# Rounded products that walk their columns in pieces, with weights at another offset: a set attention with a gated feed-forward on one core

## The chip, the cores and the metric

The kernel runs on one core of one Trainium2 chip. The metric is the device time of one execution in microseconds; the time before is the median of three runs.

## The reference

```python
def mab(q, kv):
    s = scale * (q @ kv.transpose(0, 2, 1))
    s = s - s.max(-1, keepdims=True)
    a = np.exp(s)
    a /= a.sum(-1, keepdims=True) + 1e-09
    return a @ kv
h = mab(I, x)                       # 32 inducing rows against 12480 rows of x, 4 batches
out = mab(x, h)                     # 12480 rows of x against the 32 rows of h
...
h = x @ w_in                        # x: 49920 x 128, w_in: 128 x 2048
g = h * (1.0 / (1.0 + np.exp(-1.702 * h)))
return g @ w_out                    # w_out: 2048 x 128
```

All arrays are float32 (the weights are decoded on chip from 64-bit floats).

## The kernel before

The four batches are cut into six sets of 4 x 512 rows and a rest of 2 x 96. For each batch the kernel computes the 32 rows of `h`, then `h @ w_in` (32 x 2048) in two rounded halves, which stand below each other in a tile `hw`; the softmax weights of 512 rows stand as a high and a low part in a stack `st` of 128 x 512 (`left` for the rests). So the product `x @ w_in` of the feed-forward becomes one matmul of `hw` with `st` for each 128 hidden columns.

The main loop goes over blocks of 512 rows, and in each over eight groups of two hidden chunks (128 each). A group `i` has these parts:

- `hidden(i)`: two first products, weights `hw`, moving columns `st`, into a PSUM tile `ph` of 2 x 512 columns (two such tiles).
- `first(i)`: ScalarE makes `g` from `ph` with the gate; `hi`, `g` rounded to fp32r, is made by ScalarE again from `ph` or by VectorE from `g`; VectorE makes `lo = g - hi`.
- `second(i, c)`: for each chunk three second products into `pso`, in this order: `hi` with `wl`, `lo` with `wh`, `hi` with `wh`, where `wh` and `wl` are the rounded high and low part of `w_out`.

All these operands are fp32r ("rounded products"). In the first eight groups `second` uses plain fp32 instead (`g` with `whole`). The order of everything is fixed when the program is built: a planner (`Clocks`, `Meter`, `Jobs`) keeps a clock of costs per engine and chooses what comes next; the second products run up to 16 chunks behind the first. The attention of the next batch is threaded in between, in tiles `pa`, `e`, `s`, `aT` and a score of small ones (`mx`, `rs`, `m2`, `sm`, `den` and others, from the pool `psm`).

In the first batch the row sets come in the order 4, 6, 3, 0, 5, 5, 2, 1 to the products `pa<-xt,indT_sb`. For sets 4, 3, 0 and 5, whose rows are turned on the chip, these products read their columns by `xg.rearrange("c (k g i) -> c g k i", g=g, i=32)`, that is in 16 runs of 32 columns; for sets 2 and 1 in one run of 512.

Every SBUF tile from the pools on starts where the one before ends. With the sizes before, `st`, `left`, `hw`, `hi`, `lo`, `wh` and `wl` all start at 64 modulo 256 bytes, and every 128-column slice of the weights (512 bytes) does too.

Of the kernel before, what the change touches and what calls it, by code (L numbers as in the profile page):

```python
# [9 lines left out]
F32 = mybir.dt.float32  # L10
I32 = mybir.dt.int32
# [9 lines left out]
P = 128  # L21
# [36 lines left out]
WC = 512  # L58
# [6 lines left out]
S2_LATER = ((0, 6), (1, 2, 3), (4, 5))  # L65
FB = 6
WINDOW = 100.0
CHAIN = 200.0
# [5 lines left out]
class Clocks:  # L74


    def __init__(self):
        self.written, self.read, self.rings, self.before, self.port = {}, {}, {}, {}, {}
        self.halved, self.entered = {}, set()

    def apart(self, t):

        name = t.tensor.name
        self.halved[name] = [f"{name}/{k}" for k in range(-(-t.shape[-1] // WC))]
        return t

    def names(self, ap):
        name = ap.tensor.name
        if name not in self.halved:
            return [name]  # L90
        per = max(1, ap.ap[0][0] // (WC * len(self.halved[name])))
        at = ap.offset % ap.ap[0][0]
# [143 lines left out]


def width(ap):
    return math.prod(ap.shape[1:])
# [3 lines left out]
def set_attention_then_moe(ctx: ExitStack, tc, xT, x, indT, w_in, w_out, outT):  # L243
# [78 lines left out]
    pt = ctx.enter_context(tc.tile_pool(name="pt", bufs=7))  # L322
    pst = ctx.enter_context(tc.tile_pool(name="pst", bufs=G))
    phw = ctx.enter_context(tc.tile_pool(name="phw", bufs=4))
    psm = ctx.enter_context(tc.tile_pool(name="psm", bufs=3))
    ps_h = ctx.enter_context(tc.tile_pool(name="ps_h", bufs=2, space=PSUM))
# [18 lines left out]
    dve.tensor_scalar(mine, rep[:, 0, :], -scale, None, op0=ALU.mult)  # L345
    one = const.tile([1, 1], F32, name="one")
    dve.memset(one, 1.0)
    warm = const.tile([1, 1], F32, name="warm")
    act.activation(warm, one, AF.Exp)
# [3 lines left out]
    w_in_sb = [w_in_all[:, c * WC:(c + 1) * WC] for c in range(NC)]  # L353
    pww = ctx.enter_context(tc.tile_pool(name="pww", bufs=NC // 2))
    whole = {}
    wh = {}
    pwl = ctx.enter_context(tc.tile_pool(name="pwl", bufs=1))
    wl = {}
# [82 lines left out]
    def new_batch(b):  # L441
        a = SimpleNamespace(b=b, s1={}, aTs={}, col={s: k for k, s in enumerate(EARLY + LATE if b == 0 else range(NS))})
        a.mx = psm.tile([P, NS], F32, tag="mx", name="mx", bufs=2)
        a.rs = psm.tile([P, NS], F32, tag="rs", name="rs", bufs=2)
        dve.memset(a.mx, -3.0e38)
        dve.memset(a.rs, 0.0)
        return a
# [72 lines left out]
    def max_scaled(pa):  # L520

        row = psm.tile([P, M], F32, tag="row", name="row", bufs=1)
# [4 lines left out]
        nmx = psm.tile([P, 1], F32, tag="nmx", name="nmx", bufs=2)  # L527
        dve.tensor_reduce(nmx, row, axis=AX.X, op=ALU.add)
        return nmx
# [31 lines left out]
    def spread(rs1):  # L561
        rsb = psm.tile([P, P], F32, tag="rsb", name="rsb", bufs=1)
        dve.tensor_copy(rsb, rs1.broadcast_to([P, P]))
        return rsb
# [7 lines left out]
    def denominators(pa):  # L572
        den = psm.tile([P, M], F32, tag="den", name="den", bufs=1)
        dve.tensor_scalar(den, pa, 1e-9, None, op0=ALU.add)
        dve.reciprocal(den, den)
        return den

    def normalised(b, pa, den):
        hT = psm.tile([P, G, M], F32, tag="hT", name="hT", bufs=1)
# [20 lines left out]
    def second_out(s, pa):  # L600

        t0, g, w = sups[s]
        q = 32 * g
        e, slot = take("e", s)
        k = w // 32
        e = e[:, 0:w].rearrange("p (k m) -> p k m", m=M)
        dve.transpose(e[0:q].rearrange("p k m -> p (k m)"), pa[0:q, 0:w])
        m2 = psm.tile([P, BLK], F32, tag="m2", name="m2")
# [16 lines left out]
    def attention(b):  # L625
# [6 lines left out]
        for pair in S1:  # L632
# [15 lines left out]
            yield from hop(HOPS[1])  # L648
        mx1 = psm.tile([P, 1], F32, tag="mx1", name="mx1", bufs=2)
        dve.tensor_reduce(mx1, a.mx, axis=AX.X, op=ALU.max)  # L650
# [17 lines left out]
        for some in (tuple(range(4)), tuple(range(4, NS))):  # L668
# [14 lines left out]
            for s in some:  # L683
# [7 lines left out]
                yield from hop(HOPS[6])  # L691
        hu = psm.tile([P, P], F32, tag="hu", name="hu", bufs=1)
        dve.tensor_copy(hu, pa[:, 0:P])
        rs1 = psm.tile([P, 1], F32, tag="rs1", name="rs1", bufs=2)
        dve.tensor_reduce(rs1, a.rs, axis=AX.X, op=ALU.add)
# [93 lines left out]
    def hw_tile(b, c):  # L789

        if (b, c // 2) not in hws:
            hws[b, c // 2] = clocks.apart(phw.tile([P, 2 * WC], F32R, tag="hw", name="hw"))
        return hws[b, c // 2][:, c % 2 * WC:(c % 2 + 1) * WC]

# [52 lines left out]
    def normalise(e):  # L847

        q, nb = e.shape[0], e.shape[1]
        sm = psm.tile([P, BLK], F32, tag="sm", name="sm")  # L850
        dve.tensor_reduce(sm[0:q, 0:nb], e, axis=AX.X, op=ALU.add)
# [24 lines left out]
    def start(pf, pw):  # L876
# [3 lines left out]
        }  # L880
        raws["w_out", 0] = clocks.apart(pwl.tile([P, 4 * WC], I32, tag="wl", name="raw"))
        turned = {}
# [84 lines left out]
        def split():  # L967

            for c in range(0, NC, 2):
                out = wholes[c // 2]  # L970
                yield act, [out], has(*SPLIT_AT[c // 2], ("w_out", c), ("w_out", c + 1))
                wh_ = clocks.apart(pww.tile([P, 2 * WC], F32R, tag="w", name="wh"))
                act.copy(wh_, out)
                if c == 0:
                    wls = clocks.apart(pwl.tile([P, DFF], F32R, tag="wl", name="wl"))
                low = wls[:, c * WC:(c + 2) * WC]
# [57 lines left out]
        def maximum(n):  # L1034
            yield dve, [a.mx], has(*[("max", s) for s in (EARLY + LATE)[:n]])
            mx1 = psm.tile([P, 1], F32, tag="mx1", name="mx1", bufs=2)
            dve.tensor_reduce(mx1, a.mx[:, 0:n], axis=AX.X, op=ALU.max)
# [68 lines left out]
        def joining():  # L1106

            yield dve, lambda: [nmxs[ES], nmxs[NS]], has(("nmx", ES), ("nmx", NS), *[("exp", s) for s in EARLY])
            less = psm.tile([P, 1], F32, tag="less", name="less", bufs=1)
            dve.tensor_sub(less, nmxs[NS], nmxs[ES])  # L1110
            rs1 = psm.tile([P, 1], F32, tag="rs1", name="rs1", bufs=2)
            rs2 = psm.tile([P, 1], F32, tag="rs2", name="rs2", bufs=1)
            dve.tensor_reduce(rs1, a.rs[:, 0:ES], axis=AX.X, op=ALU.add)
# [13 lines left out]
            yield dve, [h12, less], has(*[("weighed", s) for s in range(NS)])  # L1127
            hu = psm.tile([P, P], F32, tag="hu", name="hu", bufs=1)
            dve.tensor_scalar(hu, h12[:, 0:P], less, None, op0=ALU.mult)
# [43 lines left out]
        def first_weights():  # L1173
# [15 lines left out]
            chain[0] = True  # L1189
            m2 = psm.tile([P, BLK], F32, tag="m2", name="m2")  # L1190
            dve.tensor_reduce(m2[:, 0:G], pa, axis=AX.X, op=ALU.max)
# [7 lines left out]
        def more_weights(e, slot):  # L1199
# [11 lines left out]
            yield dve, [e], None  # L1211
            m2 = psm.tile([P, BLK], F32, tag="m2", name="m2")
            dve.tensor_reduce(m2[:, G:], far, axis=AX.X, op=ALU.max)
# [84 lines left out]
        jobs.add(first_h_w_in(), rank("hw"))  # L1298
        temps_out = [clocks.apart(pww.tile([P, 2 * WC], U16, tag="w", name="tmp")) for _ in range(2)]
        wholes = [clocks.apart(phw.tile([P, 2 * WC], F32, tag="hw", name="whole")) for _ in range(2)]  # L1300
        for c in range(NC):
# [66 lines left out]
    def hidden(i):  # L1368
# [4 lines left out]
        for c in range(2):  # L1373
            ch = 2 * k + c
            for b, at, w, _ in of:
                pe_.matmul(
                    ph[:, c, at:at + w], hw[b, ch // 4][:, ch % 4 * P:(ch % 4 + 1) * P],
                    st[:, at:at + w], start=True, stop=True,
                )
# [17 lines left out]
    def second(i, c):  # L1397
# [185 lines left out]
```

## Time and profile before

| | |
|---|---|
| median of three runs | 1539.3 us (1538.69 to 1539.86) |
| span of the profiled execution | 1537.2 us, first to last instruction; its own time is given by this span alone, so the part around it is read as the 2.1 us to the median |
| TensorE (matmul) busy | 1529.9 us, 100% |
| TensorE (weight load) busy | 1229.4 us, 80% |
| ScalarE busy | 1345.4 us, 88% |
| VectorE busy | 1301.1 us, 85% |

A matmul's duration in the profile is a latency and overlaps with the next one, so the step from start to start is what the stream costs. Weight loads have rows of their own (PEld) and lie beside the matmul before the one that uses them. L181 is the helper that records each operation, so groups are told apart by their tiles: `pso<-hi,wl` is the tile written, the moving operand and the weights.

### The profile page before, as it was taken

The page shows a single profiled execution, that of the slowest core. Times are in us where ns is not written, and L with a number is a line of the kernel's source. Part 1 is how long each engine was busy: PE and PEld are TensorE (multiplying, and loading weights), DVE is VectorE, ACT ScalarE, POOL GpSimd, SP SyncE. Part 2 cuts the span into 40 slices and gives each one's busy share as a digit, 9 for nine tenths or more (in the row PEclk, how much of TensorE's full clock was granted, in tenths as well). Part 3 has the DMA queues.
Part 4 walks back from the last instruction along what each step waited for, and adds up shares of the span by engine and source line. Part 5 has one row for each costly group of instructions (what it writes and reads, how often), then busy time and mean ns, then how long its engine had stood idle before and what let it go on. Part 6 is the DMA issues. An engine that isn't in the chain of part 4 may idle for free.

```text
span 1537.2 us, 21743 instructions
## 1 busy us (share of the span) xinstructions
PE 1529.9 (100%) x7736; PEld 1229.4 (80%) x7736; DVE 1301.1 (85%) x1512; ACT 1345.4 (88%) x1549; POOL 0.7 (0%) x6
## 2 busy tenths in 40 slices
PE   9999999999999999999999999999999999999999
PEld 6588878877888887877787887887788888888887
DVE  7988888789788887789789888778978888888886
ACT  4899989898999888889999888989899998888884
POOL 0000000000000000000000000000000000000000
PEclk9999999999999999999999999999999999999999
DMA  8210157713051115833133110872301101101100
GB/s 335 74 50 25 49 205 124 215 40 101 31 206 42 35 35 97 180 104 102 42 102 131 39 49 14 158 200 57 97 23 40 48 25 37 49 24 40 48 26 20
DMA packets 83849, 127.53 MB, mean 83 GB/s; under 512 B 12320, under 2 KB 50848, under 8 KB 77856
## 3 DMA queue, kind: packets, MB, share of 16 engines
q1 hardware_dynamic: 83600, 126.05, 28.8%
q8 instruction: 63, 1.03, 0.3%
q14 instruction: 42, 0.34, 0.1%
q10 hardware_dynamic: 144, 0.10, 0.0%
HBM read 72.11 MB, written 25.56 MB: 64 GB/s over the span
## 4 chain that ended last, share of the span: by engine, by line
PE 97%; DMA 1%; DVE 0%; ACT 0%; issue 0%; SPq 0%
PE pso L181 69%; PE ph L181 23%; PE pa L181 4%; DMA xt<-in_xT 1%; PE h L181 0%; ACT g L181 0%; PE spun L1268 0%; DMA hw<-tl 0%; DVE e L181 0%; DVE m L181 0%; DVE sm L181 0%; DVE two L181 0%; SPq L196 0%; DVE hw L181 0%; DVE w_in_all L181 0%
## 5 line engine op out<-in xcount | busy, mean ns | idle before, releaser
L181 DVE TENSOR_TENSOR lo<-g,hi 128x1024 fp32r<-128x1024 f32 x776 | 938.0, 1216 | 136.1 <-ACT hi L181 121.8
L181 ACT ACTIVATE g<-ph 128x1024 f32<-128x1024 f32 (+1 forms) x784 | 812.8, 1042 | 153.8 <-PE ph L181 74.7
L181 PE MATMUL pso<-hi,wl 128*128 128x512 f32 (+1 forms) x1552 | 603.7, 389 | 0.0
L181 PE MATMUL pso<-lo,wh 128*128 128x512 f32 (+1 forms) x1552 | 602.4, 388 | 0.0
L181 PE MATMUL pso<-hi,wh 128*128 128x512 f32 (+1 forms) x1552 | 602.3, 388 | 0.0
L181 ACT ACTIVATE hi<-ph 128x1024 fp32r<-128x1024 f32 (+1 forms) x493 | 512.6, 1040 | 0.0
L181 PE MATMUL ph<-st,hw 128*128 128x512 f32 x1536 | 474.9, 393 | 1.1 <-ACT g L181 1.1
L181 PEld LDWEIGHTS ph<-st,hw 128*128 128x128 f32 x1536 | 285.8, 188 | 77.0 <-issue 9.1
L181 PEld LDWEIGHTS pso<-hi,wl 128*128 128x128 f32 x1552 | 291.4, 188 | 62.8 <-issue 2.5
L181 PEld LDWEIGHTS pso<-hi,wh 128*128 128x128 f32 x1552 | 291.2, 188 | 59.6
L181 PEld LDWEIGHTS pso<-lo,wh 128*128 128x128 f32 x1552 | 291.4, 188 | 59.1
L181 DVE CAST hi<-g 128x1024 fp32r<-128x1024 f32 (+1 forms) x283 | 193.5, 684 | 73.8 <-ACT g L181 73.4
L181 ACT COPY ob<-pso 128x512 f32<-128x512 f32 (+1 forms) x98 | 60.0, 612 | 11.1 <-PE pso L181 11.1
L181 ACT ACT_TABLE_LOAD x26 | 33.4, 1283 | 1.2 <-PEq L1573 0.7
L181 PE MATMUL pa<-xt,indT_sb 128*32 128x512 f32 x200 | 24.9, 599 | 0.5 <-DMA xt<-in_xT 0.4
L181 ACT ACTIVATE s<-s,nmx 128x512 f32<-128x512 f32 (+1 forms) x27 | 17.8, 662 | 4.1 <-DVE nmx L181 4.0
L181 PE MATMUL pa<-xt,hT 128*32 128x512 f32 (+1 forms) x176 | 21.3, 593 | 0.0
L181 DVE TENSOR_TENSOR e<-e,sm 128x512 f32<-128x512 f32 (+3 forms) x29 | 17.8, 612 | 1.0
L181 DVE TENSOR_REDUCE m<-e 128x16 f32<-128x512 f32 (+2 forms) x28 | 17.3, 619 | 1.0
L181 DVE STREAM_TRANSPOSE aT<-s 128x512 f32<-128x512 f32 (+1 forms) x28 | 17.8, 640 | 0.2
L181 DVE TENSOR_REDUCE sm<-e 128x16 f32<-128x512 f32 (+3 forms) x29 | 17.3, 596 | 0.4 <-ACT e L181 0.4
L181 DVE TENSOR_TENSOR e<-e,m 128x512 f32<-128x512 f32 (+2 forms) x28 | 17.3, 617 | 0.0
(120 smaller groups left out, 356.9 us busy)
## 6 DMA issues: line engine op xcount, KB each, us to landing
xt<-in_xT SPq DMA_DIRECT2D x44, 1024.0 KB, 7.6
out_T<-ob SPq DMA_DIRECT2D x96, 256.0 KB, 2.0
xn<-in_x SPq DMA_DIRECT2D x72, 256.0 KB, 7.1
st<-ahT SPq DMA_DIRECT2D x184, 64.0 KB, 2.0
st<-alT SPq DMA_DIRECT2D x184, 64.0 KB, 2.0
raw<-in_w_in SPq DMA_DIRECT2D x4, 512.0 KB, 10.8
xf<-in_x SPq DMA_DIRECT2D x2, 1024.0 KB, 17.4
raw<-in_w_out SPq DMA_DIRECT2D x4, 512.0 KB, 15.3
```

What stands on the lines that cost most here:

```text
L181: return f(*a, **k)
```

## The change

Three things are changed, and no operation is added or taken away.

1. The rounded products of `hidden` and `second` get another access pattern, `by_lines`, for the moving columns and for the output alike: pieces of 4 columns (16 bytes), each fourth piece in turn, so columns 0-3, 16-19, 32-35, ... to the end, then 4-7, 20-23, ..., four passes in all. Column k of the output still belongs to column k of the input. The plain fp32 products keep the single run.
2. The weight tiles `hw`, `wh` and `wl` get 4 spare columns (16 bytes) at either end, and the pools stand in another order. In the built program `hi` and `lo` start at 224 modulo 256, `st` and `left` at 0, the weights in `wh` and `wl` at 16, those in `hw` at 48. Thus `hi` and `lo` against `wh` and `wl`, and `st` against `hw`, lie 208 bytes behind modulo 256; `hi` against `hw` lies at 176, and `st` against `wl` at 240.
3. The small tiles come from several pools that stand between the larger ones, with as many buffers of each as before. `hw` is now one tile of 2048 columns per batch and two such tiles, instead of four of 1024.

```diff
+LINES = (4, 4)
+ASIDE = 4
+SMALL = {"m2": "psm1", "less": "psm2", "rs2": "psm4", "row": "psm4", "mx": "psm4", "den": "psm5", "rs": "psm5", "sm": "psm6"}
...
+def by_lines(ap):
+
+    return ap.rearrange("p (n s i) -> p s n i", s=LINES[0], i=LINES[1])
...
-    pst = ctx.enter_context(tc.tile_pool(name="pst", bufs=G))
-    phw = ctx.enter_context(tc.tile_pool(name="phw", bufs=4))
-    psm = ctx.enter_context(tc.tile_pool(name="psm", bufs=3))
...
+    pool_of("phw0")
+    pool_of("psm1", 3)
+    pst = pool_of("pst", G)
+    pool_of("psm2")
+    pool_of("phw1")
+    pool_of("psm3", 2)
+    pool_of("pw0")
+    pool_of("psm4", 2)
+    pool_of("pw1")
+    pool_of("psm5", 2)
+    pool_of("pwl")
+    pool_of("psm6", 3)
+    pools["psm5"].tile([P, 8], F32, tag="aside", name="aside", bufs=1)
...
+    def aside(pool, tag, name, n):
+        t = clocks.apart(pools[pool].tile([P, n * WC + 2 * ASIDE], F32R, tag=tag, name=name), ASIDE)
+        return t[:, ASIDE:ASIDE + n * WC]
...
-        if (b, c // 2) not in hws:
-            hws[b, c // 2] = clocks.apart(phw.tile([P, 2 * WC], F32R, tag="hw", name="hw"))
-        return hws[b, c // 2][:, c % 2 * WC:(c % 2 + 1) * WC]
+        if b not in hws:
+            hws[b] = aside(f"phw{b % 2}", f"hw{b % 2}", "hw", 4)
+        return hws[b][:, c * WC:(c + 1) * WC]
...
-                wh_ = clocks.apart(pww.tile([P, 2 * WC], F32R, tag="w", name="wh"))
+                wh_ = aside(f"pw{c // 2}", f"w{c // 2}", "wh", 2)
...
-                    wls = clocks.apart(pwl.tile([P, DFF], F32R, tag="wl", name="wl"))
+                    wls = aside("pwl", "wl", "wl", 4)
...
                 pe_.matmul(
-                    ph[:, c, at:at + w], hw[b, ch // 4][:, ch % 4 * P:(ch % 4 + 1) * P],
-                    st[:, at:at + w], start=True, stop=True,
+                    by_lines(ph[:, c, at:at + w]), hw[b, ch // 4][:, ch % 4 * P:(ch % 4 + 1) * P],
+                    by_lines(st[:, at:at + w]), start=True, stop=True,
                 )
...
-            pe_.matmul(o, wlc, hi[:, c, :], start=(ch == 0), stop=False)
-            pe_.matmul(o, whc, lo[:, c, :], start=False, stop=False)
-            pe_.matmul(o, whc, hi[:, c, :], start=False, stop=last)
+            out, high, low = by_lines(o), by_lines(hi[:, c, :]), by_lines(lo[:, c, :])
+            pe_.matmul(out, wlc, high, start=(ch == 0), stop=False)
+            pe_.matmul(out, whc, low, start=False, stop=False)
+            pe_.matmul(out, whc, high, start=False, stop=last)
```

The change moves no instruction on any engine. TensorE's order in the main loop, before (tile written, moving operand and weights, then the output's shape):

```order
L181 MATMUL pso<-hi,wh 128x512
L181 MATMUL ph<-st,hw 128x512 x2
L181 MATMUL pso<-hi,wl 128x512
L181 MATMUL pso<-lo,wh 128x512
L181 MATMUL pso<-hi,wh 128x512
L181 MATMUL pso<-hi,wl 128x512
```

The same place of the change:

```order
L185 MATMUL pso<-hi,wh 128x4x32x4
L185 MATMUL ph<-st,hw 128x4x32x4 x2
L185 MATMUL pso<-hi,wl 128x4x32x4
L185 MATMUL pso<-lo,wh 128x4x32x4
L185 MATMUL pso<-hi,wh 128x4x32x4
L185 MATMUL pso<-hi,wl 128x4x32x4
```

Only the shape differs (and the line of the recording helper): 512 columns are now 4 passes of 32 pieces of 4 columns.

## Rows read from the trace of the kernel before

**Rows 1.** The page's parts 1 and 2: busy times, and the granted TensorE clock.
```profile
PE 1529.9 (100%) x7736; PEld 1229.4 (80%) x7736; DVE 1301.1 (85%) x1512; ACT 1345.4 (88%) x1549; POOL 0.7 (0%) x6
...
PEclk9999999999999999999999999999999999999999
```
**Rows 2.** The page's part 4: the chain that ended last, shares by engine and line.
```profile
PE 97%; DMA 1%; DVE 0%; ACT 0%; issue 0%; SPq 0%
PE pso L181 69%; PE ph L181 23%; PE pa L181 4%; DMA xt<-in_xT 1%; PE h L181 0%; ACT g L181 0%; PE spun L1268 0%; DMA hw<-tl 0%; DVE e L181 0%; DVE m L181 0%; DVE sm L181 0%; DVE two L181 0%; SPq L196 0%; DVE hw L181 0%; DVE w_in_all L181 0%
```
**Rows 3.** Groups by form: names, shapes, count, busy us, mean ns, idle before.
```profile
L181 PE MATMUL pso<-hi,wl 128*128 128x512 f32 x1520 | 592.9, 390 | 0.0
...
L181 PE MATMUL ph<-st,hw 128*128 128x512 f32 x1536 | 474.9, 393 | 1.1 <-ACT g L181 1.1
...
L181 PE MATMUL pso<-hi,wl 128*128 128x384 f32 x32 | 10.8, 338 | 0.0
...
L181 PE MATMUL ph<-left,hw 128*128 128x192 f32 x64 | 9.4, 269 | 0.0
```
**Rows 4.** Pieces of the chain: start us, us, what.
```profile
1124.87 6.80 PE pso L181 x30
```
**Rows 5.** Timeline of a plain stretch: start us, us, engine, operation.
```profile
1240.06 0.39 PE L181 MATMUL pso<-lo,wh 128*128 128x512 f32 x1
...
1240.28 0.39 PE L181 MATMUL pso<-hi,wh 128*128 128x512 f32 x1
...
1240.51 0.39 PE L181 MATMUL pso<-hi,wl 128*128 128x512 f32 x1
1240.51 0.19 PEld L181 LDWEIGHTS pso<-lo,wh 128*128 128x128 f32 x1
1240.74 0.39 PE L181 MATMUL pso<-lo,wh 128*128 128x512 f32 x1
```
**Rows 6.** Timeline of TensorE in the last block, twenty products of 384 columns.
```profile
1527.02 0.33 PE L181 MATMUL pso<-lo,wh 128*128 128x384 f32 x1
...
1530.31 0.33 PE L181 MATMUL pso<-hi,wh 128*128 128x384 f32 x1
```
**Rows 7.** Timeline of TensorE, plain fp32 second products in the first groups.
```profile
63.53 2.74 PE L181 MATMUL pso<-g,whole 128*128 128x512 f32 x6
65.70 1.02 PE L181 MATMUL ph<-st,hw 128*128 128x512 f32 x2
66.56 1.02 PE L181 MATMUL pso<-g,whole 128*128 128x512 f32 x2
67.02 1.04 PE L181 MATMUL ph<-st,hw 128*128 128x512 f32 x2
```
**Rows 8.** Timeline of TensorE in the first batch: set 4, then set 2.
```profile
8.31 1.07 PE L181 MATMUL pa<-xt,indT_sb 128*32 128x512 f32 x8
...
22.55 1.07 PE L181 MATMUL pa<-xt,indT_sb 128*32 128x512 f32 x8 [0.43 <-DMA xt<-in_xT]
```
**Rows 9.** Timeline of TensorE, first products of a rest, 192 columns each.
```profile
1519.80 0.59 PE L181 MATMUL ph<-left,hw 128*128 128x192 f32 x4
1520.22 0.41 PE L181 MATMUL pso<-hi,wl 128*128 128x512 f32 x1
```
**Rows 10.** Busy times by stretch: us, PE, PEld, DVE, ACT, POOL, clock, DMA share, GB/s.
```profile
140.00:210.00 70.00, 70.00 (x319) 55.60 (x318) 58.15 (x71) 65.54 (x76) 0.00 (x0) 1.00 0.35 125
...
1200.00:1300.00 100.00, 100.00 (x442) 82.52 (x441) 86.83 (x90) 91.03 (x102) 0.00 (x0) 1.00 0.14 40
1400.00:1500.00 100.00, 100.00 (x443) 82.81 (x442) 87.61 (x99) 84.95 (x96) 0.00 (x0) 1.00 0.10 32
```
**Rows 11.** Waits: who waited for whom, us in total, times, longest us.
```profile
ACT g L181 <- PE ph L181: 74.7, 107, 2.4
...
PEld ph L181 <- ACT g L181: 6.6, 8, 1.4
```

More of the change, by code (lines that the diff above doesn't have):

```diff
@@ L78, in __init__, with apart @@
         self.written, self.read, self.rings, self.before, self.port = {}, {}, {}, {}, {}
-        self.halved, self.entered = {}, set()
-    def apart(self, t):
+        self.halved, self.entered, self.aside = {}, set(), {}
+    def apart(self, t, aside=0):
         name = t.tensor.name
-        self.halved[name] = [f"{name}/{k}" for k in range(-(-t.shape[-1] // WC))]
+        self.aside[name] = aside
+        self.halved[name] = [f"{name}/{k}" for k in range(-(-(t.shape[-1] - 2 * aside) // WC))]
         return t
@@ L91, in names @@
         per = max(1, ap.ap[0][0] // (WC * len(self.halved[name])))
-        at = ap.offset % ap.ap[0][0]
+        at = ap.offset % ap.ap[0][0] - self.aside[name] * per
         end = (at + sum(step * (n - 1) for step, n in ap.ap[1:])) // per
@@ L322, in set_attention_then_moe, with pool_of, small @@
     pt = ctx.enter_context(tc.tile_pool(name="pt", bufs=7))
-    pst = ctx.enter_context(tc.tile_pool(name="pst", bufs=G))
-    phw = ctx.enter_context(tc.tile_pool(name="phw", bufs=4))
-    psm = ctx.enter_context(tc.tile_pool(name="psm", bufs=3))
+    pools = {}
+    def pool_of(name, bufs=1):
+        pools[name] = ctx.enter_context(tc.tile_pool(name=name, bufs=bufs))
+        return pools[name]
+    pool_of("phw0")
[11 more added lines that the diff above has]
+    pools["psm5"].tile([P, 8], F32, tag="aside", name="aside", bufs=1)
+    def small(shape, tag, name, **k):
+        return pools[SMALL.get(tag, "psm3")].tile(shape, F32, tag=tag, name=name, **k)
+    def aside(pool, tag, name, n):
+        t = clocks.apart(pools[pool].tile([P, n * WC + 2 * ASIDE], F32R, tag=tag, name=name), ASIDE)
+        return t[:, ASIDE:ASIDE + n * WC]
     ps_h = ctx.enter_context(tc.tile_pool(name="ps_h", bufs=2, space=PSUM))
@@ L345, in set_attention_then_moe @@
     dve.tensor_scalar(mine, rep[:, 0, :], -scale, None, op0=ALU.mult)
-    one = const.tile([1, 1], F32, name="one")
+    ones = const.tile([1, 2], F32, name="ones")
+    one, warm = ones[:, 0:1], ones[:, 1:2]
     dve.memset(one, 1.0)
-    warm = const.tile([1, 1], F32, name="warm")
     act.activation(warm, one, AF.Exp)
@@ L353, in set_attention_then_moe @@
     w_in_sb = [w_in_all[:, c * WC:(c + 1) * WC] for c in range(NC)]
-    pww = ctx.enter_context(tc.tile_pool(name="pww", bufs=NC // 2))
     whole = {}
     wh = {}
-    pwl = ctx.enter_context(tc.tile_pool(name="pwl", bufs=1))
     wl = {}
@@ L442, in new_batch @@
         a = SimpleNamespace(b=b, s1={}, aTs={}, col={s: k for k, s in enumerate(EARLY + LATE if b == 0 else range(NS))})
-        a.mx = psm.tile([P, NS], F32, tag="mx", name="mx", bufs=2)
-        a.rs = psm.tile([P, NS], F32, tag="rs", name="rs", bufs=2)
+        a.mx = small([P, NS], tag="mx", name="mx", bufs=2)
+        a.rs = small([P, NS], tag="rs", name="rs", bufs=2)
         dve.memset(a.mx, -3.0e38)
@@ L520, in max_scaled @@
     def max_scaled(pa):
-        row = psm.tile([P, M], F32, tag="row", name="row", bufs=1)
+        row = small([P, M], tag="row", name="row", bufs=1)
         dve.tensor_reduce(
@@ L526, in max_scaled @@
         dve.tensor_mul(row, row, mine)
-        nmx = psm.tile([P, 1], F32, tag="nmx", name="nmx", bufs=2)
+        nmx = small([P, 1], tag="nmx", name="nmx", bufs=2)
         dve.tensor_reduce(nmx, row, axis=AX.X, op=ALU.add)
@@ L561, in spread @@
     def spread(rs1):
-        rsb = psm.tile([P, P], F32, tag="rsb", name="rsb", bufs=1)
+        rsb = small([P, P], tag="rsb", name="rsb", bufs=1)
         dve.tensor_copy(rsb, rs1.broadcast_to([P, P]))
@@ L572, in denominators @@
     def denominators(pa):
-        den = psm.tile([P, M], F32, tag="den", name="den", bufs=1)
+        den = small([P, M], tag="den", name="den", bufs=1)
         dve.tensor_scalar(den, pa, 1e-9, None, op0=ALU.add)
@@ L578, in normalised @@
     def normalised(b, pa, den):
-        hT = psm.tile([P, G, M], F32, tag="hT", name="hT", bufs=1)
+        hT = small([P, G, M], tag="hT", name="hT", bufs=1)
         dve.tensor_mul(
@@ L607, in second_out @@
         dve.transpose(e[0:q].rearrange("p k m -> p (k m)"), pa[0:q, 0:w])
-        m2 = psm.tile([P, BLK], F32, tag="m2", name="m2")
+        m2 = small([P, BLK], tag="m2", name="m2")
         yield e, slot
@@ L648, in attention @@
             yield from hop(HOPS[1])
-        mx1 = psm.tile([P, 1], F32, tag="mx1", name="mx1", bufs=2)
+        mx1 = small([P, 1], tag="mx1", name="mx1", bufs=2)
         dve.tensor_reduce(mx1, a.mx, axis=AX.X, op=ALU.max)
@@ L691, in attention @@
                 yield from hop(HOPS[6])
-        hu = psm.tile([P, P], F32, tag="hu", name="hu", bufs=1)
+        hu = small([P, P], tag="hu", name="hu", bufs=1)
         dve.tensor_copy(hu, pa[:, 0:P])
-        rs1 = psm.tile([P, 1], F32, tag="rs1", name="rs1", bufs=2)
+        rs1 = small([P, 1], tag="rs1", name="rs1", bufs=2)
         dve.tensor_reduce(rs1, a.rs, axis=AX.X, op=ALU.add)
@@ L849, in normalise @@
         q, nb = e.shape[0], e.shape[1]
-        sm = psm.tile([P, BLK], F32, tag="sm", name="sm")
+        sm = small([P, BLK], tag="sm", name="sm")
         dve.tensor_reduce(sm[0:q, 0:nb], e, axis=AX.X, op=ALU.add)
@@ L880, in start @@
         }
-        raws["w_out", 0] = clocks.apart(pwl.tile([P, 4 * WC], I32, tag="wl", name="raw"))
+        raws["w_out", 0] = clocks.apart(pools["pwl"].tile([P, 4 * WC], I32, tag="wl", name="raw"))
         turned = {}
@@ L1035, in maximum @@
             yield dve, [a.mx], has(*[("max", s) for s in (EARLY + LATE)[:n]])
-            mx1 = psm.tile([P, 1], F32, tag="mx1", name="mx1", bufs=2)
+            mx1 = small([P, 1], tag="mx1", name="mx1", bufs=2)
             dve.tensor_reduce(mx1, a.mx[:, 0:n], axis=AX.X, op=ALU.max)
@@ L1108, in joining @@
             yield dve, lambda: [nmxs[ES], nmxs[NS]], has(("nmx", ES), ("nmx", NS), *[("exp", s) for s in EARLY])
-            less = psm.tile([P, 1], F32, tag="less", name="less", bufs=1)
+            less = small([P, 1], tag="less", name="less", bufs=1)
             dve.tensor_sub(less, nmxs[NS], nmxs[ES])
-            rs1 = psm.tile([P, 1], F32, tag="rs1", name="rs1", bufs=2)
-            rs2 = psm.tile([P, 1], F32, tag="rs2", name="rs2", bufs=1)
+            rs1 = small([P, 1], tag="rs1", name="rs1", bufs=2)
+            rs2 = small([P, 1], tag="rs2", name="rs2", bufs=1)
             dve.tensor_reduce(rs1, a.rs[:, 0:ES], axis=AX.X, op=ALU.add)
@@ L1127, in joining @@
             yield dve, [h12, less], has(*[("weighed", s) for s in range(NS)])
-            hu = psm.tile([P, P], F32, tag="hu", name="hu", bufs=1)
+            hu = small([P, P], tag="hu", name="hu", bufs=1)
             dve.tensor_scalar(hu, h12[:, 0:P], less, None, op0=ALU.mult)
@@ L1189, in first_weights @@
             chain[0] = True
-            m2 = psm.tile([P, BLK], F32, tag="m2", name="m2")
+            m2 = small([P, BLK], tag="m2", name="m2")
             dve.tensor_reduce(m2[:, 0:G], pa, axis=AX.X, op=ALU.max)
@@ L1211, in more_weights @@
             yield dve, [e], None
-            m2 = psm.tile([P, BLK], F32, tag="m2", name="m2")
+            m2 = small([P, BLK], tag="m2", name="m2")
             dve.tensor_reduce(m2[:, G:], far, axis=AX.X, op=ALU.max)
@@ L1298, in start @@
         jobs.add(first_h_w_in(), rank("hw"))
-        temps_out = [clocks.apart(pww.tile([P, 2 * WC], U16, tag="w", name="tmp")) for _ in range(2)]
-        wholes = [clocks.apart(phw.tile([P, 2 * WC], F32, tag="hw", name="whole")) for _ in range(2)]
+        temps_out = [
+            clocks.apart(pools[f"pw{k}"].tile([P, 2 * WC], U16, tag=f"w{k}", name="tmp")) for k in range(2)
+        ]
+        both = clocks.apart(pools["phw1"].tile([P, 4 * WC], F32, tag="hw1", name="whole"))
+        wholes = [both[:, 2 * k * WC:2 * (k + 1) * WC] for k in range(2)]
         for c in range(NC):
```

## The prediction

> **What bounds the kernel now.** I read the page's busy times first. TensorE is busy for the whole span and its granted clock is full, 2.4 GHz, in all forty slices [rows 1]. That alone says little, because matmul ends are modelled. So I went on to the chain that ended last: 97% of the span lies on TensorE, 69% on the second products into `pso` and 23% on the first products into `ph` [rows 2]. The forms behind those shares are few: 1520 of 512 columns for each of the three second products, 1536 first products, 32 of each second product with 384 columns, and 64 first products with 192 [rows 3]. That makes 4560 + 96 + 1536 + 64 = 6256 rounded products, and they are what the change touches.
>
> The mean of one (390 ns) is a latency. What counts is the step from one start to the next, and the timeline and the chain show it. Thirty second products of 512 columns take 6.80 us on the chain [rows 4], so 226.7 ns each, and the single starts agree: 1240.06, 1240.28, 1240.51, 1240.74 [rows 5]. The rows also show which load runs beside which product: with the product by `wl` starts the load of `wh` for the product after it. At 384 columns the starts go from 1527.02 to 1530.31 in 19 steps, 173.2 ns each [rows 6]. The two steps differ by 53.5 ns for 128 columns, 0.418 ns a column, which is one column per 2.4 GHz cycle (0.417 ns). So 512 columns need 213.3 ns and **13.3 ns of each step do not depend on the columns**: 32 column times. One weight load brings 128 columns of 4 bytes, 512 bytes, or 32 pieces of 16 bytes. One lost column per piece would give just this number. That is a reading, not a proof.
>
> A second row speaks for it. Each plain fp32 product `pso<-g,whole` has two records, and each has 512 columns. Six records need 2.17 us up to the next first product, two need 0.46 [rows 7]: (2.17 - 0.46)/4 = 427.5 ns, and two streams of 512 columns would take 426.7. About 1 ns is left over (up to 3 ns by the rounding of the starts), though a load of the same 512 bytes runs below each. So a load beside a stream need not cost 13 ns. It does where the stream takes a new column in each cycle.
>
> **The change, part by part.** The order of instructions and their waits stay on all engines; no DMA is added or moved. Three things are left.
>
> (1) The addresses. Before, all rounded operands start at the same place modulo 256, so the stream and the load beside it walk from the same offset. Now the columns lie 208 bytes behind the weights. But the load beside a product is that of the next one. By the order of the program, 4787 products have a load at 208 beside them, 717 (from `hi` with `wh` to `hw`) at 176, and 708 (from `st` or `left` with `hw` to `wl`) at 240. The other 44 stand ahead of smaller jobs.
>
> (2) The walk: 128 pieces of 4 columns in place of one run of 512, on the reading and on the writing side.
>
> (3) Small tiles in other places, with as many buffers as before. I cost this at nothing: no engine waits for them on the chain [rows 2], and if a small tile came late, its chain has the other products of the order as cover.
>
> The price of (1) and (2) together is in no row. The bounds for a step: all 13.3 ns gone (no stall left) on the one side. On the other side, a loss: if every one of the 128 pieces costs one column time more, 128 x 0.417 = 53 ns are added. The nearest row for a stepped walk is in the first batch: the products `pa<-xt,indT_sb` of set 4 read their columns in 16 runs of 32, those of set 2 in one run, and eight records need 1.07 us in both cases [rows 8]. That speaks for zero on the reading side, but with runs eight times as long, in fp32, and with an unbroken output. For the stall itself the nearest row is the fp32 pair, with 1 to 3 ns left over [rows 7]. So I take 2 ns as the rest for the 4787 products at 208: 4787 x 11.3 ns = 54 us. For the 717 + 708 at other offsets I know only 0 to 13.3 and take half: 1425 x 6.7 ns = 9.5 us. The 64 products of 192 columns give nothing either way; four of them take 0.42 us, 105 ns each [rows 9], more than their 80 ns of streaming, so the load sets their pace. (They also show that a load can follow a load after 105 ns; at 215 ns a step the loads are no bound.) Together 63.5 us.
>
> What is late next? ScalarE is busy 65.5 of 70 us in the stretch with the largest share, 93.6%, and 91.0 and 85.0 of 100 in the plain stretches behind [rows 10]. All 13.3 ns would shrink a stretch by 5.9%, my forecast by 4.5%. So ScalarE has room in each, but little in the first. It also waits for `ph` now, 74.7 us in all, and gets part of that back [rows 11]. Against that, the loads for `ph` wait 6.6 us for ScalarE's `g` [rows 11], and this grows when TensorE comes sooner. I add 6 us, about as much again; the bounds I keep are 0 and 20 us, three times the 6.6.
>
> The sum: -54 - 9.5 + 6 = -57.5 us. The profiled execution's span is 1537.2, 2.1 us under the median of 1539.3; I take those 2.1 us as unchanged. 1539.3 - 57.5 = **1482 us**.
>
> **Two rules of the skill against this.** In [rows 5] the load and the stream overlap and the step is 13.3 ns longer than the stream. The Trainium skill ("TensorE: Matmul & The Clock Gate", Step-by-step: what each phase is for) says that the stream and the weight load have SBUF read ports of their own, so that a load takes nothing from the running product. By that rule addresses cannot matter and the sum would be 0 us; the 13.3 ns next to the 1 ns of the fp32 pair speak against it, but do not show that an address is the reason.
>
> The second bears on the writing side. All outputs of TensorE in this trace are unbroken runs. The Trainium skill ("Advanced Engine Details and Errata", PSUM Cachelines) says that an access pattern that is not contiguous in PSUM slows matmuls significantly, and also that two neighbouring elements should be contiguous for the best rate. By its first half this change loses; by its second, runs of four are enough. No row here shows either.
>
> **The rivals.**
> - *Nothing moves.* The 13.3 ns belong to a rounded product or to its load at any address. For it: they are the same at 384 and 512 columns, and every pair in this trace has the same offset, so none shows another price. Against it: the fp32 pair. Time: 1539.
> - *A part.* Other offsets still meet, only at other moments: a third to a half of the stall goes. 6192 x 4.4 to 6.7 ns = 27 to 41 us; with few new waits some 1500 to 1515.
> - *All of it.* 6192 x 13.3 = 82 us, 1457, and with 6 us of waits 1463.
> - *Slower: the broken writes.* Each run of 4 columns in PSUM (or each step to another piece in SBUF) costs one column time. 6192 x 53.3 ns = 330 us; even if the stall goes as forecast, 1539 + 330 - 64 = 1805. For it: no output in this trace is broken. Against it: [rows 8], for the reading side. The point that decides is low: 10.3 ns of mean gain over 128 pieces is 0.08 ns a piece, a fifth of a column time. A whole column time for each piece is likely, if there is any cost; between, little.
>
> **How the numbers follow.** Most of the stall gone (1463 to 1500): 0.50, because the number 32 and the fp32 pair both point to the load meeting the stream. A part (1500 to 1536): 0.27. Nothing: 0.09. Slower: 0.14. About 0.2% (3 us) is what a measurement of this kernel can tell from no change. So faster 0.77, same 0.09, slower 0.14. The range goes from 1460, all of the stall gone and few new waits, up to 1541, which takes in the case of no change; it leaves out the slower case and a little below. The likeliest case alone has 1463 to 1500.
>
> **What would show it.** In the changed profile, runs of `pso` on the chain should show about 215 ns a product (30 in 6.45 us) where they had 6.80, and the 384-column steps about 162 ns. The pairs at 176 and 240 can be read apart: the step from `hi` with `wh` to `ph`, and from `ph` to `wl`. ScalarE's waits for `ph` should shrink from 74.7 us and TensorE's waits for `g` grow by a few. Wrong would be: a step that still has 226.7 (no contention by address); one that grows with the columns by over 0.418 ns (the walk costs per piece); or steps of 215 with the time lost again in waits for ScalarE.

## The result and the profile after

The changed kernel takes 1517.5 us (median of 4 runs, 1517.05 to 1518.42) against 1539.2 us (median of the four runs of the kernel before beside them): 21.7 us less, ratio 0.986 (95% interval 0.9845 to 0.9873). The forecast was 1482. The sign was right, the size was 2.6 times too large.

The busy times of the changed kernel, against [rows 1], and its chain, against [rows 4]:

```profile
PE 1507.8 (99%) x7736; PEld 1226.8 (81%) x7736; DVE 1300.5 (86%) x1512; ACT 1343.5 (89%) x1549; POOL 0.7 (0%) x6
```

```profile
1109.31 6.63 PE pso L185 x30
```

The work of VectorE and ScalarE is the same to 2 us, and TensorE has 22 us less. Thirty second products on the chain need 6.63 us, 221.0 ns each, where they had 226.7. That is less than half of the 13.3 ns of each step that do not depend on the columns. The timeline of a plain stretch (start us, us, engine, operation; TensorE alone) shows where the rest goes, against [rows 5]:

```profile
1243.53 0.38 PE L185 MATMUL pso<-hi,wl 128*128 128x512 f32 x1
1243.75 0.38 PE L185 MATMUL pso<-lo,wh 128*128 128x512 f32 x1
1243.97 0.38 PE L185 MATMUL pso<-hi,wh 128*128 128x512 f32 x1
1244.19 0.38 PE L185 MATMUL pso<-hi,wl 128*128 128x512 f32 x1
1244.41 0.38 PE L185 MATMUL pso<-lo,wh 128*128 128x512 f32 x1
1244.63 0.39 PE L185 MATMUL pso<-hi,wh 128*128 128x512 f32 x1
1244.85 0.62 PE L185 MATMUL ph<-st,hw 128*128 128x512 f32 x2
1245.32 0.38 PE L185 MATMUL pso<-hi,wl 128*128 128x512 f32 x1
```

Between second products the starts step by 0.22. The two first products together take 0.47, 1244.85 to 1245.32, where two steps of before are 0.45. So the second products gained and the first products lost. The table is taken from all starts of the two traces, by what a step goes from and to, with the offset of the pair in brackets (means over all steps, the few long waits included):

| step, 512 columns | count | before, ns | after, ns | difference, us |
|---|---|---|---|---|
| second to second product (208) | 3850 | 227.3 | 221.0 | -24.3 |
| second to first (176) | 710 | 226.9 | 225.6 | -1.0 |
| first to first (208) | 800 | 236.0 | 236.7 | +0.6 |
| first to second (240) | 693 | 227.1 | 231.8 | +3.3 |
| products of 384 and 192 columns, others | | | | -0.2 |
| sum | | | | -21.6 |

The sum is the difference of the spans, 1537.2 - 1515.5 = 21.7 us. The means hide how even the steps are. Of 808 products by `wl` that follow another second product, 798 step by 220 ns. In a group of the usual form the step from the last second product to `ph` is 226, from the first `ph` to the second 229, from there to `wl` 232 or 233, and the one after that 218. In cycles of 2.4 GHz 220.0 ns is 528: 16 above the 512 columns, where 226.7 was 32 above.

The products of 384 columns, against [rows 6]:

```profile
1505.09 0.33 PE L185 MATMUL pso<-lo,wh 128*128 128x384 f32 x1
...
1508.25 0.33 PE L185 MATMUL pso<-hi,wh 128*128 128x384 f32 x1
```

19 steps in 3.16 us are 166.3 ns (173.2 before): again some 16 column times above 160.0. The walk in pieces adds nothing per column.

### The profile page after: what moved, and what is told of

It reads as the page before. It is cut to its first block, busy times and chain, and to the rows that moved or that the text cites. A ratio compares the mean times of both kernels' runs of the same rounds, so it can differ in the third digit from the quotient of the medians.

```text
span 1515.5 us, 21743 instructions
## 1 busy us (share of the span) xinstructions
PE 1507.8 (99%) x7736; PEld 1226.8 (81%) x7736; DVE 1300.5 (86%) x1512; ACT 1343.5 (89%) x1549; POOL 0.7 (0%) x6
## 4 chain that ended last, share of the span: by engine, by line
PE 98%; DVE 1%; DMA 1%; ACT 0%; issue 0%; SPq 0%
PE pso L185 69%; PE ph L185 24%; PE pa L185 4%; PE h L185 0%; PE spun L1299 0%; DMA xt<-in_xT 0%; ACT g L185 0%; DMA hw<-tl 0%; DVE e L185 0%; DVE sm L185 0%; ACT s L185 0%; DVE m L185 0%; DVE two L185 0%; DVE aT L185 0%; DVE hw L185 0%
## 5 line engine op out<-in xcount | busy, mean ns | idle before, releaser
L185 PE MATMUL pso<-hi,wh 128*128 128x512 f32 (+1 forms) x1552 | 593.8, 383 | 0.0
L185 PE MATMUL pso<-hi,wl 128*128 128x512 f32 (+1 forms) x1552 | 590.2, 380 | 0.0
L185 PE MATMUL pso<-lo,wh 128*128 128x512 f32 (+1 forms) x1552 | 589.6, 380 | 0.0
```

The lines of the kernel that those rows point to most:

```text
L185: return f(*a, **k)
```

## The experiments

Six kernels ran. Three are the kernel with one part of the change altered, three are rounded products alone, to price a step without anything beside it.

**A sweep of walks and offsets** (`sweep`). A step is the time from one product's start to the next. The offset is the number of bytes, modulo 256, by which the columns lie behind the weights that are loaded beside them; a walk is the order in which a product reads its columns. The core of it:

```diff
+    def group(k, s, i, d, how="both"):
+        mv = m[:, d // 4:d // 4 + 512]
...
+        for r in range(N):
+            c = r % 4
+            nc.tensor.matmul(b, w[:, c * P:(c + 1) * P], a, start=(r == 0), stop=(r == N - 1))
```

> This kernel computes nothing of the reference: it runs only rounded products of 512 columns, 16 in a row for each setting, all from one weight tile and one column tile. It steps the columns' offset behind the weights from 0 to 240 bytes modulo 256 in steps of 16, for nine walks: one run of 512, then pieces of 4 columns taken each 2nd, 4th, 8th, 16th and 32nd, pieces of 8 taken each 4th, pieces of 16 taken each 2nd and each 4th; and, for pieces of 4 taken each 4th, the same walk on the reading side alone and on the writing side alone. Theory A (the stream and the load beside it meet at addresses modulo 256): at offset 0 one run gives 226.7 ns a step as in the kernel before, pieces of 4 taken each 4th at 208 give 220 ns as in the second products after the change, and for both walks the step changes by several ns with the offset; writing alone in pieces changes nothing. Theory B (the walk alone sets the step): within a walk all offsets give the same, 226.7 for one run and 220 for pieces of 4 taken each 4th, and the part of the walk that matters can be the writing side.

Mean of the last 12 steps of each setting, in ns, from the starts in the trace. The first setting, one run at offset 0, began at the lower of the clock's two levels, 1.2 GHz, with steps of 427 ns, and is left out; its value is that of the setting "written in pieces, read in one run", which reads the same.

```
offset       0     16    32    48    64    80    96    112   128   144   160   176   192   208   224   240
one run      228.6 231.7 233.2 233.3 229.7 231.2 234.2 231.1 231.7 233.3 233.9 231.1 233.3 234.4 233.3 226.7
4, each 4th  223.3 224.4 224.9 222.3 220.0 230.0 230.0 228.2 230.0 224.2 226.6 223.5 227.4 220.0 226.7 229.9
```

For the other walks, the lowest and the highest of their 16 offsets: pieces of 4 taken each 2nd 231.1 to 233.4, each 8th 240.0 to 249.7, each 16th 276.5 to 279.8, each 32nd 264.8 to 270.8; pieces of 8 each 4th 224.4 to 235.2; pieces of 16 each 2nd 230.0 to 242.2, each 4th 232.7 to 239.2. Reading in pieces and writing in one run gives the second line again, within 0.1 ns at 15 of 16 offsets (at 32 it gave 220.8 for 224.9). Writing in pieces and reading in one run gives the first line at all 15 that can be compared.

So Theory A holds and B falls: offset and walk both count, the step goes from 220.0 to 280 ns, and 64 and 208 share the floor. The four slices of the weights lie 512 bytes apart and step alike at 64 and 208; that 256 bytes more make no difference was not tried by itself. **What lies on the writing side costs nothing** in this walk: pieces of 16 bytes in PSUM, each 4th in turn, read 0.0 ns longer than one run. The rival that ended slower falls here, by its own mechanism; its price of one column time per piece would have been 53 ns. The Trainium skill ("Advanced Engine Details and Errata", PSUM Cachelines) says both that a non-contiguous pattern slows matmuls and that two neighbours should be contiguous. This trace agrees with the second: runs of four show 0.0 ns. Shorter runs were not tried on the writing side alone.

**The walk alone** (`walk_alone`), the kernel before with `by_lines` and nothing else:

```diff
-                    ph[:, c, at:at + w], hw[b, ch // 4][:, ch % 4 * P:(ch % 4 + 1) * P],
-                    st[:, at:at + w], start=True, stop=True,
+                    by_lines(ph[:, c, at:at + w]), hw[b, ch // 4][:, ch % 4 * P:(ch % 4 + 1) * P],
+                    by_lines(st[:, at:at + w]), start=True, stop=True,
...
+            out, high, low = by_lines(o), by_lines(hi[:, c, :]), by_lines(lo[:, c, :])
```

> The kernel before with the walk of the change alone; all offsets stay 0. Theory A (address and walk together): the step of the second products is not 220 ns, and the first products are equal to the second, since all pairs have one offset; the time lies anywhere from 1505 to 1560 us. Theory B (walk alone): second products at 220 ns, and the first products as slow as in the changed kernel (229 and 232 ns), so 1517 us.

Measured: 1534.7 us, ratio 0.997 (0.9958 to 0.9978). Its nine times spread over 4.3 us (1531.1 to 1535.4), those of before over 1.8. Pieces of the chain and starts in the timeline:

```profile
753.32 6.81 PE pso L181 x30
...
389.64 6.79 PE pso L181 x30
```

```profile
1241.43 0.39 PE L181 MATMUL pso<-hi,wl 128*128 128x512 f32 x1
1241.66 0.38 PE L181 MATMUL pso<-lo,wh 128*128 128x512 f32 x1
1241.88 0.39 PE L181 MATMUL pso<-hi,wh 128*128 128x512 f32 x1
...
1243.01 0.40 PE L181 MATMUL pso<-hi,wh 128*128 128x512 f32 x1
1243.25 0.39 PE L181 MATMUL pso<-hi,wl 128*128 128x512 f32 x1
```

Thirty products need as long as before, 227 ns each, but the steps are uneven: 0.23, 0.22, 0.24. The walk alone is worth 4.4 us. First and second products are alike, as Theory A had it: 226 ns in the mean from second to second, to the first and back (between two first products 234 ns, and 236 in the kernel before, waits included).

The starts in the trace show more than the mean. The steps run in one of two repeating orders, and one order holds for hundreds of products:

```
815.8 us on, 581 steps, mean 223.3    218 230 224 221 218 230 224 221 219 230 224 221 ...
448.8 us on, 575 steps, mean 226.6    220 222 221 234 239 225 226 220 222 221 234 239 225 226 ...
```

Some 4800 of 6040 steps are in the order of seven (226.7), some 1000 in the order of four (223.3, the sweep's value for this walk at 0). What chooses between them was not found.

**The offsets alone** (`offset_alone`), the changed kernel with

```diff
-    return ap.rearrange("p (n s i) -> p s n i", s=LINES[0], i=LINES[1])
+    return ap
```

> The changed kernel with its addresses, but each product reads and writes one run of 512 columns. Theory A in the form that the offset alone removes the stall: 1517 us, second products at 220 ns. Theory B: 226.7 ns in all and 1539 us. Between: a step that differs with the pair, 208, 176 and 240.

Measured: 1576.9 us, ratio 1.025 (1.0232 to 1.0262), slower than either kernel. Both expectations missed: neither the gain nor no change. The chain:

```profile
772.71 7.00 PE pso L185 x30
```

233.3 ns a step. The sweep's first line has it: one run at 208 gives 234.4, and only at 0 and 240 does it come to 226.7 (at 0 after some nine products). The kernel before stood at one of the two best of the 16 offsets for one run. So the two parts do not add: walk -4.4, offsets +37.9, both -21.7 us.

**All pairs at 208** (`all_208`). 32 bytes of small tiles move, so the stack starts at 224 and the weights in `hw` at 16:

```diff
     pool_of("psm3", 2)
+    pools["psm3"].tile([P, 8], F32, tag="more", name="more", bufs=1)
...
-    pools["psm5"].tile([P, 8], F32, tag="aside", name="aside", bufs=1)
+    spare = pools["psm5"].tile([P, 8], F32, tag="aside", name="aside", bufs=1)
...
-    ones = const.tile([1, 2], F32, name="ones")
+    ones = spare[0:1, 0:2]
```

> The changed kernel with 32 bytes moved, so that the stack starts at 224 and the first products' weights at 16 modulo 256: now every stream lies 208 bytes behind the weights loaded beside it, also at the changes from second to first products and back, which lie at 176 and 240 in the changed kernel. Theory A (the pair's offset sets the step): the three steps round a pair of first products (225.6, 229.0 and 232.3 ns in the changed kernel) come to 220 to 221 each, some 25 ns for each of 700 pairs, 17 us: about 1500 us. Rival (a change of the tile read, or the first write of a bank, costs this at any offset): the three steps stay as they are, 1517 us.

Measured: 1500.1 us (1499.9 to 1501.4), ratio 0.975 to the kernel before (0.9735 to 0.9764), 17.4 us below the changed kernel. Busy times, chain, and the same stretch of the timeline:

```profile
PE 1491.9 (99%) x7736; PEld 1227.8 (82%) x7736; DVE 1299.9 (87%) x1512; ACT 1342.4 (90%) x1549; POOL 0.7 (0%) x6
```

```profile
738.81 6.60 PE pso L185 x30
```

```profile
1243.51 0.38 PE L185 MATMUL pso<-hi,wl 128*128 128x512 f32 x1
...
1244.61 0.38 PE L185 MATMUL pso<-hi,wh 128*128 128x512 f32 x1
1244.83 0.60 PE L185 MATMUL ph<-st,hw 128*128 128x512 f32 x2
1245.27 0.38 PE L185 MATMUL pso<-hi,wl 128*128 128x512 f32 x1
```

The two first products now take 0.44 us instead of 0.47, and 220 ns is the common step of all kinds (608 of 701 first to first, 585 of 652 from there to `wl`). The step from the first `ph` to the second had 208 in the changed kernel already, and still it falls from 229 to 220. So the pair's own offset doesn't set its step alone: what stood before it counts. This is also the version that beats both kernels.

But even with all pairs at 208 the step is not always 220. From 987.16 to 997.81 us, 45 products with all pairs at 208 and no other product between them step by 236.7 ns each, and the order ends only with the stretch:

```profile
987.16 0.40 PE L185 MATMUL pso<-hi,wl 128*128 128x512 f32 x1
987.40 0.40 PE L185 MATMUL pso<-lo,wh 128*128 128x512 f32 x1
...
997.81 0.40 PE L185 MATMUL pso<-hi,wh 128*128 128x512 f32 x1
```

So here too one layout has more than one order of steps. It is the only long stretch of this kind in this trace; what holds it there is open.

**Weights, fine offsets, history** (`sweep2`).

```diff
+        if kind == "one":
+            return w[:, c * P:c * P + 1].broadcast_to([P, P])
+        if kind == "half":
+            return w[:, c * P:c * P + 64]
...
+    for d in (64, 208):
+        for other in range(0, 256, 16):
+            group(4, 4, [d] * 5 + [other] + [d] * 10)
```

> Again rounded products of 512 columns alone, 16 in a row for each setting, nothing of the reference. First the weights: 128 weight columns side by side, one weight column read 128 times (one 16-byte piece to fetch), 64 columns, and 128 columns taken each second and each fourth (64 and 128 pieces), for one run of 512 and for pieces of 4 taken each 4th, at offsets 0, 64, 144 and 208. Theory A (each piece of weights that is fetched takes time from the stream): one weight column and one run of 512 come near 214 ns, 64 columns to 220 (half of 13.3), each fourth column goes well above 230. Rival (a rounded product costs the same whatever its load reads): 220 to 234 ns in all of these. Second, offsets in steps of 4 bytes between the 16-byte ones for pieces of 4: by theory A some change against the neighbours, none below 220 expected. Third, four other walks at 16 offsets: nothing below 220 expected. Fourth, history: 16 products at 64 or 208 with one other offset in the sixth place, and the order of the changed kernel, 176, 208, 240 among 208: if a step depends on what came before it, the product at 208 behind the one at 176 takes 229 ns as in the changed kernel, and the disturbance lasts more than one step; by the rival that a pair has its price, each product at 208 takes 220.

From the starts in the trace, mean of the last 11 steps at offsets 0, 64, 144, 208 (the first value of the first line fell in the lower clock level):

```
weights                     one run                      pieces of 4, each 4th
128 columns           -      229.2  233.3  234.6         223.3  223.2  220.0  220.1
one column, 128 times 230.9  231.5  235.8  229.2         221.5  226.7  226.9  226.5
64 columns            229.6  228.5  231.5  226.6         219.7  223.5  229.6  221.5
each second           233.4  233.2  231.1  233.3         223.6  223.1  223.2  222.7
each fourth           234.5  238.7  233.4  236.7         238.4  237.1  238.4  237.5
```

Here the reading "one lost column for each of 32 pieces of weights" falls. A load that reads one column 128 times over still leaves 221 to 236 ns, not the 214 expected, and half the weights leave 220 to 232. The place of the weights matters (the line for one column differs from that for 128 at the same offset), their amount hardly does until each column has a piece of its own (each fourth: 233 to 239).

At offsets between the 16-byte ones a product read in pieces of 4 takes 445 to 453 ns, twice as long, and pieces of 2 columns, each 4th, take 460 to 462 at every offset. The Trainium skill ("Advanced Engine Details and Errata", SBUF Cachelines) says that at least two hits on a 16-byte line are needed to absorb the access latency. Here two were not enough: the pieces of 2 have two columns in a line, and at 8 bytes past a line each piece of 4 has two columns in each of two lines; that step is 447 to 450 ns. No setting's mean in 13 walks and five ways of reading the weights went below 219.7.

History, steps in ns; the sixth product has another offset:

```
208, sixth at 48    220 220 220 220 220 222 223 221 229 231 221 220 220 220 220 220
208, sixth at 128   220 220 220 220 220 225 227 230 230 220 220 221 220 220 220 220
 64, sixth at 80    220 220 220 220 220 234 239 226 224 228 223 217 221 224 228 223
 64, sixth at 64    220 220 220 220 220 220 220 220 220 220 220 220 220 220 220 220
```

One odd product among products at 208 disturbs up to eight steps. All 15 disturbances at 208 ended, and the step came back to 220; at 64 some did not within ten products, and the setting can also run at 222 and 225 in turn (the 223.2 above, where the first sweep had 220.0). So both offsets have the floor, but in this run only 208 came back to it each time; the stretch at 236.7 in the kernel shows that even 208 need not.

The order 176, 208, 240 among products at 208 was run too: 220 220 224 222 228 218 220. The product at 208 behind the one at 176 takes 222 ns, where 229 was expected from the changed kernel (226, 229, 232, 218). It is slower than 220, so the steps before count. But the distances are the same as in the changed kernel and the steps are not: here the columns move and the weights stay, there both move. So while the steps are disturbed, the distance of a pair isn't all that counts.

**The main loop's order without the rest** (`pattern`).

```diff
+            for c in range(2):
+                for q, (m, t) in enumerate((("hi", "wl"), ("lo", "wh"), ("hi", "wh"))):
+                    nc.tensor.matmul(
+                        walk(o, s, i), cut(t, w, P, (r + c) % 3), walk(cut(m, hi, 512), s, i),
+                        start=(r == c == q == 0), stop=(r == 7 and c == 1 and q == 2),
+                    )
+            for c in range(2):
+                nc.tensor.matmul(
+                    walk(ph[:, c], s, i), cut("hw", hw, P, c), walk(cut("st", st, 512), s, i), start=True, stop=True
+                )
```

> Rounded products of 512 columns alone, nothing of the reference. First 16 settings with pieces of 4 taken each 4th in which the columns stay 208 bytes behind the weights and both are moved together by 0 to 240 bytes. Theory A (the distance of stream and weights counts): 220 ns in all 16. Rival (the place of the stream itself counts): it changes with the shift. Then the order of the main loop, six second products and two first ones, eight times over, in seven layouts: that of the kernel before with one run (226.7 in all), that of the changed kernel (225.6, 229.0, 232.3 round the first products, 218 to 220 else), all at 208 (220 in all), only the first products' weights moved, so that the pairs round the first products lie at 208, 240, 240, only the stack moved (176, 176, 208), all at 64, and all at 0 with pieces. Theory A with history: wherever all pairs are equal at 208 or 64 the steps are 220; the two half-moved layouts lose something again; all at 0 with pieces shows no fixed step, 218 to 231. Rival (a change of tile or bank costs): the steps round the first products stay near 225 to 232 in every layout with pieces.

Columns at 208 behind the weights and both moved together: 220.0 or 220.1 in all 15 settings at the full clock (mean of the last 11 steps). Where all pairs are alike, the distance counts, not the place. The order of the main loop in the layout of the changed kernel, with no other engine at work:

```profile
88.98 0.38 PE L63 MATMUL pso<-hi,wl 128*128 128x512 f32 x1
89.20 0.38 PE L63 MATMUL pso<-lo,wh 128*128 128x512 f32 x1
89.42 0.38 PE L63 MATMUL pso<-hi,wh 128*128 128x512 f32 x1
89.64 0.38 PE L63 MATMUL pso<-hi,wl 128*128 128x512 f32 x1
89.86 0.38 PE L63 MATMUL pso<-lo,wh 128*128 128x512 f32 x1
90.08 0.39 PE L63 MATMUL pso<-hi,wh 128*128 128x512 f32 x1
90.31 0.62 PE L68 MATMUL ph<-st,hw 128*128 128x512 f32 x2
90.77 0.38 PE L63 MATMUL pso<-hi,wl 128*128 128x512 f32 x1
```

It repeats the changed kernel's steps within a nanosecond. The layouts, mean step and one period of eight (six second products, two first ones):

```
kernel before, one run     226.7   227 226 227 227 226 226 228 226
changed kernel             223.1   218 220 221 220 220 226 229 232
all at 208                 220.0   220 220 220 220 220 219 221 220
weights of ph at 16 alone  222.3   223 225 221 220 220 219 221 231
stack at 224 alone         224.9   222 225 221 220 220 225 239 228
all at 64                  220.0   220 220 220 220 220 220 220 220
all at 0, in pieces        223.3   224 223 223 224 223 222 225 223
```

Neither a change of tile nor a first write of a bank costs anything: with all pairs at 208 they are 220. In the changed kernel it is the mixture of offsets that costs. All at 0 in pieces, for which no fixed step was expected, gives 222 to 225, mean 223.3, where the kernel with the walk alone has 226. That kernel's own trace has the reason: most of its steps are in the order of seven, at 226.7, and it keeps to this order for 575 steps with no product of the attention between them.

## Why the prediction was wrong

**The bound was right.** TensorE's stream sets the time, and the gain came out of the 13.3 ns alone. That half of them (226.7 to 220.0) hangs on where stream and load lie is shown by the sweep; where the other half lies is not. The order was untouched, and the small tiles cost nothing that the busy times show.

**The rest at 208 was mis-sized.** The step that failed: "So I take 2 ns as the rest for the 4787 products at 208: 4787 x 11.3 ns = 54 us." The rest is 6.7 ns in the even steps (220.0) and 7.7 in the mean of the second products (221.0), and the gain is 24.4 us (24.3 of the second products, 0.7 of those with 384 columns, less 0.6 of the first products), 5.1 ns for each of the 4787. That is 30 us too much. The fp32 pair [rows 7] was the wrong neighbour: it shows what a load leaves where each column has two cycles, and no setting of rounded products of 512 columns with a full load came below 220 in the mean in any of 13 walks. The reading of 32 pieces of weights, which made the pair seem fit, fell in the second sweep.

**The other offsets gained nothing.** "For the 717 + 708 at other offsets I know only 0 to 13.3 and take half" had 9.5 us of gain; they lost 2.3 (-1.0 and +3.3). The bounds had left a loss out for them, though the working before it had a loss in its list. The first products at 208 belong here too: counted at 11.3 ns each, they got 2 ns slower in the usual group, because the pairs round them are odd. That a step depends on the steps before it was in none of the rivals.

**The waits for ScalarE did not come.** I added 6 us. TensorE's time without work went from 7.3 to 7.7 us (span less busy), and the waits for it hardly moved, against [rows 11] and, for the last line, against this one of the kernel before:

```profile
PEld ph L181 <- ACT hi L181: 2.4, 5, 0.8
```

The changed kernel:

```profile
ACT g L185 <- PE ph L185: 68.0, 103, 2.3
...
PEld ph L185 <- ACT g L185: 6.5, 10, 1.4
...
PEld ph L185 <- ACT hi L185: 3.5, 10, 0.8
```

ScalarE still has room where its share is largest, against [rows 10]: 65.4 of 69 us, 94.8%.

```profile
138.00:207.00 69.00, 69.00 (x320) 55.66 (x319) 58.06 (x71) 65.41 (x76) 0.00 (x0) 1.00 0.35 121
```

The terms close: -57.5 forecast, +29.7 for the rest at 208, +11.8 for the other offsets, -5.6 for the waits, gives -21.6. (The 4787 and 1425 also hold the 64 products of 192 columns, which the prediction gives nothing; that is under 1 us.)

**The rivals.** "A part" was the right one (the time lies 2.5 us above its 1500 to 1515), but its reason, other offsets that still meet, fits at most the steps round the first products. "Nothing moves" and the rule of the Trainium skill ("TensorE: Matmul & The Clock Gate", Step-by-step: what each phase is for) that a load takes nothing from the running product fell: with the same walk and no other engine at work, the step changes by 10 ns with the distance between stream and weights and not with their common place. For the other half of the 13.3 ns "nothing moves" is not refuted, since 220 ns is the lowest step of a full load at any address tried. "Slower by broken writes" fell in the sweep.

## What to carry to other kernels

Where rounded products follow each other without a gap, look at the step from start to start and compare it with the columns: a constant above them can hang on where the columns lie behind the weights that are loaded beside them, which are those of the next product. Change walk and offset together, give every pair in the order the same distance, the ones at the seams included, and choose a distance at which a disturbed step comes back; then look in the kernel's own trace for stretches where it did not. And price such a change by a run of products alone before pricing it by a neighbour row: 170 us of them repeated the steps of the kernel before, the changed one and the one at 208 within a nanosecond or two. With the walk alone they showed another order than the kernel, so a mean of 16 products is one order of steps and need not be the only one.

## What was not expected of the hardware

- A step depends on the steps before it. Settings run into a fixed step (226.7 for one run at 0 and 240, 220.0 for pieces at 64 and 208) or wander between 218 and 242 in a repeating order. One setting can have more than one: pieces at 0 have 223.3 and 226.7, at 64 220.0 and 223.2, at 208 220.0 and, in one stretch of 45 products, 236.7. A single odd product shows for up to eight steps at 208 and for ten and more at 64.
- Offsets alone, with the runs unbroken, cost 6.6 ns a step (1576.9 us): the kernel before was at one of the two best offsets tried for its walk without a sign of it in its profile.
- A piece of 4 columns that does not start on a 16-byte line doubles the step, 445 to 453 ns.
- What the last 16 column times of the 220 ns are was not found. They stay, in the mean of a setting, with one weight column, with 64, and at every walk and offset tried. No run left the load out, so whether they belong to the load or to the product itself is open.
